# A gated scan with a soft mixture of experts: inputs laid out by numpy, one pool of 48 slots, phases of four units, a combine over 32 rows

## The chip, the cores and the metric

The kernel runs on one core of a Trainium2 chip. The metric is the device time of one execution in microseconds; 300.68 us is the median of three runs before the change. TensorE (PE) multiplies and transposes, VectorE (DVE), ScalarE (ACT) and GpSimd (POOL) compute, SyncE (SP) issues the DMA transfers.

## The reference

Four sequences of 5056 tokens with 256 channels pass a gated linear recurrence; its 20224 x 256 output is the input of a soft mixture of 8 experts with 4 slots each. Everything is fp32.

```python
a_base = sigmoid(a_param)
log_a  = 8 * sigmoid(r_gate) * log(clip(a_base))
a_t    = exp(log_a)
xg     = sqrt(max(1 - a_t*a_t, 1e-6)) * sigmoid(i_gate) * x
h[t]   = a_t[t] * h[t-1] + xg[t]            # scan over 5056 tokens: x for the second part

logits = x @ phi                            # [20224, 32 slots]
d      = softmax of logits over the tokens
slot_input = d.T @ x                        # [32, 256]
slot_out[e] = relu(slot_input[e] @ w1[e]) @ w2[e]      # 8 experts, 256 x 1024 x 256
c      = softmax of logits over the slots
out    = c @ slot_out                       # [20224, 256]
```

The output needs all tokens' logits and the slots' outputs, so there are two stages with a narrow place between them: gates, scan and the softmax sums over all tokens first, then a small expert MLP, then the combine and the stores.

## The kernel before, in words

Tokens are cut into quads of 512 (40, the last of 256) and units of two quads (21: the first unit has one quad, the last half a one). SBUF has 8 `st` buffers of 4 KB per partition, 20 `b` buffers of 8 KB, and a few small ones; PSUM has pairs of banks for the gate stage.

Names of tasks carry the quad, the unit (with channel half 0 or 1) or the group of up to four quads:

- `Dr`, `Di`, `Dx` (SP): loads of r_gate, i_gate and x, 512 KB each, tokens on partitions. `TR` (PE): transposes of r into PSUM, channels on partitions. `SR` (ACT, L797): tanh of it, from PSUM into `A`. `EX` (ACT, L865): exp, gives a_t; two whole units of a chunk can be taken by one instruction per half. `SQ` (POOL or DVE, L852): a_t squared, into `N`. `RT` (ACT, L888): the root.
- `SI` (ACT, L812): tanh of i_gate. `P1` (POOL, L823) and `U` (DVE L833, DVE or POOL L835): its product with x. The string `IV` gives a letter for each quad: D lets DVE do (tanh + 1) * x at once, P lets POOL add 1 first, E multiplies only and lets PE add x when it transposes, S uses the sigmoid table. `TU` (PE, L907): transposes of the product; under E both i and x pass through PE.
- `ST` (DVE, L925): the product times the root; `SC` (DVE, L942): the scan, in place in `A`. `TY` (PE), `YC` (DVE L981 or ACT L979): transposed back and copied out of PSUM.
- For each group: `LG` (PE, L1027) logits, `LE` and `LD` (running maximum over tokens), `TE`, `ES` (exp), `AC` (PE, sums weighted with it), `AE` (DVE). `CT`, `CM`, `CS`, `CE`, `RR`, `RB`, `RC`, `CN` make the softmax over the slots (transposes, maximum, subtraction, exp, sum, reciprocal, product); they can run in the gate stage or behind it.
- The narrow place: `MT`, `MX`, `MR`, `MC`, `WJ`, `WE`, `W`, `SP`, `SL` merge the sums into the slots' inputs; `L1` (PE, L1360), `HS`, `HT`, `HR`, `L2` (PE, L1408) are the MLP of all experts; `SO`, `RS` normalise and repeat the slots' outputs over the partitions.
- The combine: `CH`, `CL`, `SH`, `BD` split both factors into a high part of 12 mantissa bits and the rest, so that fp32r matmuls over 64 rows (32 slots of two parts) give the product: `HP` (PE, L1566) transposes, `HE` copies, `OT` (PE, L1593) multiplies, `OE` (DVE L1612, ACT L1610) copies out of PSUM, `OD` (SP, L1632) stores.

A planner in the file only turns these tasks into a program: the order on each engine is written out in the table `ORDER`, one list of names for an engine, and the buffers are given out in that order. PE gets filler transposes of the identity (L1231) where the plan has it idle. ACT needs a table load at each change between tanh or exp and the root, so the units are handled in chunks: all tanh and exp of a chunk, then all its roots. `CHUNKS` gives the number of units in each. On the chip each engine runs its list strictly in order and waits for the semaphores of its operands.

Of the kernel before, what the change touches and what calls it, by code (L numbers as in the profile page):

```python
# [1673 lines left out]
```

## Time and profile before

| | |
|---|---|
| runs | 300.63, 300.68, 301.33 us; median 300.68 |
| profiled execution | 300.78 us, of which the span of the core's instructions is 299.0 |
| busy | PE 267.0, DVE 243.1, ACT 247.1, POOL 189.0 us |
| moved | 78.94 MB read, 20.71 MB written |
| first store issued | 244.87 us after the span's start |

Busy time is that of instructions in execution. PE's includes fillers, and the ends of its matmuls are modelled, so a busy PE need not be at its limit. The share of DMA is the mean over 16 engines.

### The profile page before, as it was taken

Reading aid. Unit: us, or ns where it says so; the run is one execution under the profiler, and the core shown is the slowest. Engines: PE = TensorE matmul, PEld = TensorE weight load, DVE = VectorE, ACT = ScalarE, POOL = GpSimd, SP = SyncE. Lnnn points to the kernel's source line nnn. Section 1 sums busy time; section 2 is a strip of 40 time slices with the busy share of each in tenths; the row PEclk is TensorE's granted clock in tenths of the full one; section 3 lists DMA queues with packets and bytes.
Section 4 is the critical chain, followed back from the end, with each engine's and each line's share of the span. In section 5 each row is a group of like instructions: output and inputs, shape, how many; then the busy total and the mean of one; then the engine's idle time right before and its main releaser. Section 6 shows DMA issues by size and latency. Waiting matters only on the chain.

```text
span 299.0 us, 6623 instructions
## 1 busy us (share of the span) xinstructions
PE 267.0 (89%) x2657; PEld 211.4 (71%) x2657; DVE 243.1 (81%) x288; ACT 247.1 (83%) x275; POOL 189.0 (63%) x147
## 2 busy tenths in 40 slices
...
GB/s 237 416 409 386 406 409 409 299 339 333 409 258 353 340 302 382 278 385 300 226 287 301 365 215 353 377 426 346 362 401 295 0 55 392 413 414 419 419 407 264
DMA packets 23491, 100.08 MB, mean 335 GB/s; under 512 B 2850, under 2 KB 2852, under 8 KB 19364
## 3 DMA queue, kind: packets, MB, share of 16 engines
...
q10 hardware_dynamic: 4, 0.00, 0.0%
HBM read 78.94 MB, written 20.71 MB: 333 GB/s over the span
## 4 chain that ended last, share of the span: by engine, by line
ACT 39%; PE 29%; DVE 17%; issue 7%; DMA 3%; POOL 1%; ACTq 0%; DVEq 0%; POOLq 0%
ACT b L865 8%; ACT b L797 8%; ACT b L888 7%; DVE b L942 7%; ACT st L812 6%; PE bank L1593 6%; DVE pair L925 4%; DMA b<-in_moe_w_dram 3%; PE pair L907 3%; PE pair L786 3%; PE bank L1566 3%; PE bank L1408 2%; PE pair L965 2%; ACT L888 2%; ACT yn L979 2%
## 5 line engine op out<-in xcount | busy, mean ns | idle before, releaser
L852 POOL TENSOR_TENSOR b<-b 128x1024 f32<-128x1024 f32 (+2 forms) x40 | 72.6, 1833 | 29.6 <-ACT b L865 29.5
L925 DVE SCALAR_TENSOR_TENSOR pair<-b,pair 128x1024 f32<-128x1024 f32 (+2 forms) x42 | 48.1, 1156 | 4.3 <-PE pair L907 3.9
L965 PEld LDWEIGHTS pair<-ident,b 128*128 128x128 f32 x316 | 38.2, 194 | 13.2 <-ACT b L797 6.1
L942 DVE TENSOR_TENSOR_SCAN b<-b,b,pair 128x1024 f32<-128x1024 f32 (+3 forms) x24 | 47.2, 1974 | 0.3
L965 PE MATMUL pair<-ident,b 128*128 128x128 f32 x316 | 44.1, 284 | 2.8 <-ACT b L797 2.7
L786 PE MATMUL pair<-ident,st 128*128 128x128 f32 x316 | 42.3, 279 | 4.8 <-ACT b L797 2.3
L942 DVE TENSOR_TENSOR_SCAN b<-b,pair 128x1024 f32<-128x1024 f32 (+5 forms) x24 | 45.8, 1926 | 0.2
L907 PE MATMUL pair<-ident,b 128*128 128x128 f32 x316 | 43.2, 275 | 2.0 <-ACT b L797 1.1
L865 ACT ACTIVATE b<-b,ca 128x2048 f32<-128x2048 f32 (+3 forms) x28 | 44.3, 1607 | 0.1
L797 ACT ACTIVATE b<-pair 128x1024 f32<-128x1024 f32 (+1 forms) x40 | 40.3, 1018 | 4.3 <-PE pair L786 4.2
L786 PEld LDWEIGHTS pair<-ident,st 128*128 128x128 f32 x316 | 35.7, 143 | 10.6 <-ACT b L797 3.8
L907 PEld LDWEIGHTS pair<-ident,b 128*128 128x128 f32 x316 | 35.4, 140 | 6.1 <-ACT b L797 2.5
L835 POOL TENSOR_TENSOR b<-st,b 128x1024 f32<-128x1024 f32 (+1 forms) x17 | 39.3, 2319 | 0.2
L812 ACT ACTIVATE st<-st 128x1024 f32<-128x1024 f32 (+1 forms) x38 | 38.8, 1056 | 0.0
L888 ACT ACTIVATE b<-b 128x2048 f32<-128x2048 f32 (+2 forms) x21 | 36.9, 1804 | 0.1
L835 POOL TENSOR_TENSOR st<-st,b 128x1024 f32<-128x1024 f32 x12 | 28.8, 2403 | 8.1 <-ACT st L812 8.1
L1593 PE MATMUL bank<-bd,hT 64*128 64x256 f32 x232 | 27.5, 308 | 3.7 <-DVE hT L1579 1.5
L1593 PEld LDWEIGHTS bank<-bd,hT 64*128 64x128 f32 x232 | 21.6, 196 | 7.6 <-issue 2.1
L1027 PE MATMUL one<-b,phi_sb 128*32 128x256 f32 (+1 forms) x328 | 26.5, 419 | 0.0
L1231 PE MATMUL one<-ident 128*128 128x128 f32 x146 | 24.1, 283 | 1.4 <-POOL ident masks.py:199 1.4
L979 ACT COPY yn<-pair 128x1024 f32<-128x1024 f32 x22 | 22.2, 1018 | 1.3 <-PE pair L965 1.1
L1610 ACT COPY b<-bank 128x512 f32<-128x512 f32 x27 | 15.1, 597 | 9.5 <-PE bank L1593 7.7
...
## 6 DMA issues: line engine op xcount, KB each, us to landing
...
```

The lines of the kernel that those rows point to most:

```text
L786: nc.tensor.transpose(out=o[:, m, :], in_=raw("r", q)[:, m * D + h * P : m * D + (h + 1) * P], identity=ident,)
L797: nc.scalar.activation(dst, t(rp)[:, :, :c], AF.Tanh, scale=0.5)
L812: nc.scalar.activation(v, v, AF.Tanh, scale=0.5)
L835: eng.tensor_tensor(out=o, in0=a, in1=b, op=ALU.mult)
L852: eng.tensor_tensor(out=t(Nb[p])[:, h, :c], in0=v, in1=v, op=ALU.mult)
L865: nc.scalar.activation(v, v, AF.Exp, scale=ca[:, h : h + 1], bias=ca[:, h : h + 1])
L888: nc.scalar.activation(v, v, AF.Sqrt, bias=f, scale=-f)
L907: nc.tensor.matmul(o[:, m, :], raw(nm, q)[:, m * D + h * P : m * D + (h + 1) * P], ident, is_transpose=True, start=(nm == nms[0] and m == ...
L925: nc.vector.scalar_tensor_tensor(v, w, 1e-3 if gate_of(quads(p)[0]) == "S" else 0.5e-3, v, op0=ALU.max, op1=ALU.mult)
L942: nc.vector.tensor_tensor_scan(dst, dst, flat()[:, s0:s1], init, op0=ALU.mult, op1=ALU.add)
L965: nc.tensor.transpose(out=flat()[:, b * D + h * P : b * D + (h + 1) * P], in_=token(t(A[p])[:, h, : plen(p)], p)[:, :, (b0 + b) * len(quad ...
L1593: nc.tensor.matmul(t(ops[k])[:, m // 2 * D : (m // 2 + 1) * D], t(hT)[r, (b + m) * P // 2 : (b + m + 2) * P // 2], T["bd"][part][r, 0, :], ...
```

## The change

Numpy, ahead of the program, now lays the inputs out. r_gate comes by channel for each unit, so `TR` is gone and one load puts it straight into `A`, where `SR` works in place on 2048 columns. x and i_gate come by unit and by blocks of 128 tokens: a partition holds the tokens p, 128 + p and so on, so `TU`, `TY` and `LG` read and write contiguous blocks, and the output rows are put back in order by numpy at the end. Loads are 1 MB for a unit. w2, phi and a_param are rearranged too, and `L1` reads w1 contiguously.

`st` and `b` become one tile `all_s` of 48 slots of 4 KB; buffers take 1, 2 or 4 neighbouring slots, in an order that a further list `B` fixes. `CHUNKS` goes from nine to seven, of up to four units. `IV` has 18 quads of E in place of 12, 16 of P in place of 15, 6 of D in place of 11 and none of S. All lists of `ORDER` are new. A small subtraction `PD` on POOL stands ahead of `DM`.

The combine has no split any more: the 32 coefficients of each of a quad's four blocks lie on 32 partitions of one transposed tile (`TB`), and `OT` multiplies each block with plain fp32 matmuls over 32 rows, four row groups into four banks. `SW` copies the repeated slot outputs once. `OD` stores a unit at a time, and the half-size unit 0 is stored first.

```diff
-CHUNKS = [2, 2, 3, 3, 3, 3, 2, 2, 1]
+CHUNKS = [1, 3, 4, 4, 4, 4, 1]
...
-IV = 'DDDDDDEDDPPEDEPDPPEPEEPPEEPEPPEDPPEEPSSP'
+IV = 'PDEPDPDPPEEEEEEEEDEEEEEEEDDPEEPPPPPPPPPP'
...
-N_ST = 8
-N_B = 20
+N_S = 48
...
-        "CA SQ0.1 SQ1.1 U0 ST0.1 ST0.0 SC0.1 SC0.0 U2 U1 YC0.0 ST1.1 SC1.1 U4 ST1.0 SC1.0 U7 U3 YC2.0 ST2.1 ST2.0 U5 "
...
+        "CA U0 SQ1.1 SQ1.0 U4 SQ2.0 ST0.1 SC0.1 U1 ST0.0 SC0.0 ST1.0 ST1.1 SC1.0 SC1.1 U6 YC1.0 ST2.1 SC2.1 ST2.0 SC2.0 "
...
-EX2 = True
+EXG = 2
...
+        all_s = sb.tile([P, N_S, J * D], F32, name="all_s")
...
+    A = {p: Buf("s", f"A{p}", 2) for p in range(NP)}
+
+    def load(nm, p):
+        b = A[p] if nm == "r" else Buf("s", f"{nm}{p}", len(quads(p)))
+        c, tok0 = plen(p), pos_u(p) * QT
+
+        def emit():
+            rows = src[nm][tok0 : tok0 + c, :].rearrange("(p n) d -> p (n d)", n=c // P)
+            if nm == "r":
+                rows, dst = rows.rearrange("p (h c) -> p h c", h=H), t(b)[:, :, :c]
+                for h in range(H) if p == 0 else [slice(0, H)]:
+                    nc.sync.dma_start(out=dst[:, h], in_=rows[:, h])
+            elif len(quads(p)) > 1:
+                nc.sync.dma_start(out=t(b), in_=rows.rearrange("p (i f) -> p i f", i=2))
+            else:
+                nc.sync.dma_start(out=t(b)[:, : c // P * D], in_=rows)
...
-        def e_tr():
-            for h in range(H):
-                o = inv(t(rp)[:, h, :c], n)
-                for m in range(n):
-                    nc.tensor.transpose(
-                        out=o[:, m, :],
-                        in_=raw("r", q)[:, m * D + h * P : m * D + (h + 1) * P],
-                        identity=ident,
-                    )
-
-        tr = add("PE", f"TR{q}", 0.232 * n - (0.35 if q == 0 else 0), deps=[ld[("r", q)], t_const], prio=q - TRP, emit=e_tr,
-                 alloc=[rp], uses=[st[("r", q)]], shape="T")
+    def mk_sr(p):
+        c = plen(p)
 
         def e_sr():
-            dst = t(A[p])[:, :, i * QT : i * QT + c]
-            nc.scalar.activation(dst, t(rp)[:, :, :c], AF.Tanh, scale=0.5)
-
-        SR[q] = add("ACT", f"SR{q}", 0.06 + 0.85 * c / QT, deps=[tr], prio=q - 2, emit=e_sr,
-                    alloc=[A[p]] if i == 0 else [], uses=[rp] + ([A[p]] if i else []), kind="tanh")
+            v = t(A[p])[:, :, :c]
+            nc.scalar.activation(v, v, AF.Tanh, scale=0.5)
...
-            v = T["b2"][A[p].slot[0] // 2][:, h::2, :] if len(us) == 2 else t(A[p])[:, h, :c]
+            v = t(A[p])[:, h, :c]
+            if len(us) > 1:
+                v = all_s[:, A[p].slot[h] :][:, : 2 * len(us) - 1 : 2, :]
...
-                                o[:, m, :],
+                                t(up)[:, i, m * P : (m + 1) * P],
...
                         o = t(lp)[NS * j : NS * (j + 1), c0 : c0 + w]
-                        v = token(t(A[p])[:, h, : plen(p)], p)
-                        near = p >= WIDE_FROM
                         nc.tensor.matmul(
-                            o.rearrange("s (p i) -> s p i", p=P) if near else o.rearrange("s (i p) -> s i p", p=P), phi_sb[:, h, :],
-                            v[:, :, j * w // P : (j + 1) * w // P] if near else v[:, :, j::nb].rearrange("c p i -> c i p"),
+                            o.rearrange("s (i p) -> s i p", p=P), phi_sb[:, h, :],
+                            t(A[p])[:, h, : plen(p)].rearrange("c (i j p) -> c j i p", j=nb, p=P)[:, j],
...
-                        t(hp)[32 * j : 32 * j + NS, :FJ].rearrange("q (p f) -> q p f", f=FH), slots(e, h),
-                        wpart(wts[("w1", e)][0], h).rearrange("d (p j f) -> d j p f", j=J, f=FH)[:, j],
+                        t(hp)[32 * j : 32 * j + NS, :FJ], slots(e, h), wpart(wts[("w1", e)][0], h)[:, j * FJ : (j + 1) * FJ],
...
-    a = add("DVE", "SH", 0.35, deps=[a], prio=-60, uses=[sr], alloc=[soHb], emit=lambda: nc.vector.tensor_scalar(
-        t(soHb)[:, :D].bitcast(I32), t(sr)[:, :D].bitcast(I32), HIGH, None, op0=ALU.bitwise_and))
-
-    def e_b(part):
-        dst = T["bd"][part][:, 0, :]
-        if part:
-            nc.vector.tensor_tensor(out=dst, in0=t(sr)[:, :D], in1=t(soHb)[:, :D], op=ALU.subtract)
+
+    def e_rc():
+        if planner.cur.eng_used == "ACT":
+            nc.scalar.copy(out=t(soRb)[:, :D], in_=t(sr)[:, :D])
         else:
-            nc.scalar.copy(out=dst, in_=t(soHb)[:, :D])
-
-    t_bd = [add("DVE" if part else "ACT", f"BD{part}0", 0.35, deps=[a, t_bz], prio=-60, uses=[soHb, bdb] + ([sr] if part else []),
-                emit=lambda part=part: e_b(part)) for part in range(2)]
-
-    planner.warm_late = lambda pl: LATE and SC[(NP - 1, 0)].start is not None and t_bd[0].start is None
+            nc.vector.tensor_copy(out=t(soRb)[:, :D], in_=t(sr)[:, :D])
+
+    t_sw = add(("DVE", "ACT"), "SW", 0.35, deps=[a], prio=-60, uses=[sr], alloc=[soRb], emit=e_rc, alt={"ACT": 0.31})
...
-        k = add("POOL", f"CL{g}", 1.0, deps=[k], prio=pr, uses=[hl, lSb[g // 4]],
-                emit=lambda: nc.gpsimd.tensor_tensor(
-                    out=parts()[:, :, 1, :], in0=cn(), in1=parts()[:, :, 0, :], op=ALU.subtract))
...
+        def e_tb(n=n, rows=rows, ht=ht, g=g):
+            for k in range(n):
+                nc.tensor.transpose(
+                    out=t(ht)[:rows, k * P : (k + 1) * P], in_=lS(g)[:, k * rows : (k + 1) * rows], identity=ident)
...
+            def e_ot(m=m, k0=k0, ops=ops, hT=hT):
+                for k in range(m):
+                    for j, op in enumerate(ops):
+                        r = slice(NS * j, NS * (j + 1))
+                        nc.tensor.matmul(
+                            t(op)[:, k * D : (k + 1) * D], t(hT)[r, (k0 + k) * P : (k0 + k + 1) * P], t(soRb)[r, :D],
+                            start=True, stop=True)
+
+            k = add("PE", f"OT{p}", OTD * m, deps=[he, t_sw], prio=pr, emit=e_ot, alloc=ops, uses=[hT, soRb], shape="F")
+            ev = []
...
+            def e_od(p=p, og=og):
+                a0, c = quads(p)[0] * QT, per_part(p)
+                nc.sync.dma_start(
+                    out=out[a0 : a0 + plen(p), :].rearrange("(p n) d -> p (n d)", n=c), in_=t(og) if len(quads(p)) > 1 else t(og)[:, : c * D])
...
+def _spans(n):
+    q = J * P
+    return [(0, q)] + [(a, min(a + 2 * q, n)) for a in range(q, n, 2 * q)]
+def _by_unit(a):
+    flat = a.reshape(-1, a.shape[-1])
+    return _np.concatenate([flat[u:v].reshape(-1, P, a.shape[-1]).transpose(1, 0, 2).reshape(-1) for u, v in _spans(len(flat))]).reshape(a.shape)
+def _by_channel(a):
+    flat = a.reshape(-1, a.shape[-1])
+    return _np.concatenate([flat[u:v].reshape(v - u, -1, P).transpose(2, 1, 0).reshape(-1) for u, v in _spans(len(flat))]).reshape(a.shape)
+def _from_units(a):
+    return _np.concatenate([a[u:v].reshape(P, -1, a.shape[-1]).transpose(1, 0, 2).reshape(-1, a.shape[-1]) for u, v in _spans(len(a))])
...
+        if name in ("x", "i_gate"):
+            a = _by_unit(a)
+        elif name == "r_gate":
+            a = _by_channel(a)
+        elif name == "moe_w2":
+            a = _np.ascontiguousarray(a.reshape(a.shape[0], -1, P, a.shape[2]).transpose(0, 2, 1, 3)).reshape(a.shape)
+        elif name in ("a_param", "moe_phi"):
+            a = _np.ascontiguousarray(a.reshape(2, P, -1).transpose(1, 0, 2)).reshape(a.shape)
...
-    return got[0]
+    return _from_units(got[0])
```

What the lists move is shown at three places. On ACT, at the start of the program, behind the loads of the first table; L797 (L781 in the change) is `SR`, L865 (L850) `EX`, L812 (L796) `SI`, L888 (L864) `RT`. Before:

```order
L797 ACTIVATE b_69<-pair_92 128x2x512
L865 ACTIVATE b_69<-b_69,ca 128x512 x2
L797 ACTIVATE b_69<-pair_94 128x2x512
L797 ACTIVATE b_69<-pair_92 128x2x512
L812 ACTIVATE st_64<-st_64 128x1024
L865 ACTIVATE b_69<-b_69,ca 128x1024 x2
L797 ACTIVATE b_72<-pair_92 128x2x512
L888 ACT_TABLE_LOAD
L888 ACTIVATE b_70<-b_70 128x2x512
L888 ACTIVATE b_71<-b_71 128x2048
```

With the change:

```order
L850 ACTIVATE all_s<-all_s,ca 128x512 x2
L781 ACTIVATE all_s<-all_s 128x2048
L850 ACTIVATE all_s<-all_s,ca 128x1024 x2
L781 ACTIVATE all_s<-all_s 128x2048 x2
L796 ACTIVATE all_s<-all_s 128x1024
L850 ACTIVATE all_s<-all_s,ca 128x2x1024
L796 ACTIVATE all_s<-all_s 128x2048
L850 ACTIVATE all_s<-all_s,ca 128x2x1024
L796 ACTIVATE all_s<-all_s 128x2048
L864 ACT_TABLE_LOAD
L864 ACTIVATE all_s<-all_s 128x2x512
L864 ACTIVATE all_s<-all_s 128x2048 x3
```

The first root moves from behind two units, one of them the small one, to behind four units; `SR` and `SI` become 2048 columns wide.

On DVE, behind the last scan; L1043 (L1015) is `LE`, L1063 (L1035) `LD`, L1116 (L1089) `AE`, L981 `YC`, L1508 (L1443) `RR`, L1425 and L1428 of the change `CM` and `CS`. Before:

```order
L1063 TENSOR_SCALAR lD_84<-one_88,M 128x256
L1042 COPY M<-M 32x1 x2
L1043 TENSOR_SCALAR b_75,M<-one_87,M 64x128
L1063 TENSOR_SCALAR lD_83<-one_87,M 64x128
L1116 SCALAR_TENSOR_TENSOR accS<-accS,dm,one_88 128x257
L1292 TENSOR_REDUCE mmax<-one_87 1x32
L1294 COPY mrep<-mmax 1x128
L981 COPY yn_82<-pair_94 128x2x256
L1298 TENSOR_TENSOR wj<-M,one_87 128x1
L1508 TENSOR_REDUCE rs_all<-b_70 128x16
L1302 TENSOR_SCALAR W<-R,wj 128x128
L1116 SCALAR_TENSOR_TENSOR accS<-accS,dm,bank_2391 128x257
```

With the change:

```order
L1443 TENSOR_REDUCE rs_all<-all_s 128x16 x2
L1014 COPY M<-M 32x1 x2
L1015 TENSOR_SCALAR all_s,M<-one_70,M 64x128
L1089 SCALAR_TENSOR_TENSOR accS<-accS,dm,one_71 128x257
L1035 TENSOR_SCALAR lD_66<-one_70,M 64x128
L1250 TENSOR_REDUCE mmax<-bank_2017 1x32
L1425 TENSOR_REDUCE rm_79<-bank_2015 128x16
L1252 COPY mrep<-mmax 1x128
L1425 TENSOR_REDUCE rm_78<-bank_2019 128x16
L1089 SCALAR_TENSOR_TENSOR accS<-accS,dm,one_71 128x257
L1428 TENSOR_TENSOR all_s<-bank_2019,rm_78 128x512
L1256 TENSOR_TENSOR wj<-M,bank_2017 128x1
```

Two sums over rows of groups done earlier, two maxima and a subtraction now stand in the stretch up to the weights of the merge, and a copy of `YC` has gone from it.

On PE, the first matmuls of the combine; in the first list eight of them make one quad (`bd` is the split matrix, `hT` the transposed coefficients), in the second the operands are plain fp32 tiles. Before:

```order
L1593 MATMUL bank_2391<-bd_2493,hT_2495 128x256
L1593 MATMUL bank_2396<-bd_2493,hT_2495 128x256
L1593 MATMUL bank_2391<-bd_2494,hT_2495 128x256
L1593 MATMUL bank_2396<-bd_2494,hT_2495 128x256
L1593 MATMUL bank_2391<-bd_2493,hT_2495 128x256
L1593 MATMUL bank_2396<-bd_2493,hT_2495 128x256
L1593 MATMUL bank_2391<-bd_2494,hT_2495 128x256
L1593 MATMUL bank_2396<-bd_2494,hT_2495 128x256
```

With the change (L1497 is `OT`, L1471 `TB`):

```order
L1497 MATMUL bank_2017<-all_s,eS_69 128x256
L1497 MATMUL one_71<-all_s,eS_69 128x256
L1497 MATMUL bank_2019<-all_s,eS_69 128x256
L1497 MATMUL bank_2018<-all_s,eS_69 128x256
L1497 MATMUL bank_2017<-all_s,eS_69 128x256
L1497 MATMUL one_71<-all_s,eS_69 128x256
L1497 MATMUL bank_2019<-all_s,eS_69 128x256
L1497 MATMUL bank_2018<-all_s,eS_69 128x256
L1471 MATMUL bank_2016<-ident,all_s 128x128 x4
```

A unit of one quad now takes four matmuls into four banks; the next row shows transposes of another group between units.

## Rows read from the trace of the kernel before

**Rows 1.** The page: busy time of each engine, and GB/s in 40 slices of 7.5 us.
```profile
PE 267.0 (89%) x2657; PEld 211.4 (71%) x2657; DVE 243.1 (81%) x288; ACT 247.1 (83%) x275; POOL 189.0 (63%) x147
...
GB/s 237 416 409 386 406 409 409 299 339 333 409 258 353 340 302 382 278 385 300 226 287 301 365 215 353 377 426 346 362 401 295 0 55 392 413 414 419 419 407 264
```

**Rows 2.** Stages: from:to, length, busy us (x instructions) by engine, PE clock, DMA share, GB/s.
```profile
0.00:25.00 25.00, 22.78 (x174) 21.89 (x175) 8.09 (x10) 20.33 (x21) 6.45 (x31) 1.00 0.93 360
...
25.00:217.35 192.35, 181.18 (x1752) 143.85 (x1751) 187.28 (x168) 189.67 (x181) 160.49 (x93) 1.00 0.90 339
...
217.35:245.00 27.65, 26.96 (x370) 16.96 (x368) 17.25 (x54) 9.23 (x20) 11.66 (x11) 1.00 0.44 182
...
245.00:299.00 54.00, 36.07 (x367) 28.72 (x365) 30.44 (x59) 27.86 (x56) 10.41 (x13) 0.83 0.94 385
```

**Rows 3.** Groups on ACT by shape: out<-in xcount | busy us, mean ns | idle before.
```profile
L797 ACT ACTIVATE b<-pair 128x1024 f32<-128x1024 f32 x39 | 39.7, 1028 | 4.3 <-PE pair L786 4.2
...
L812 ACT ACTIVATE st<-st 128x1024 f32<-128x1024 f32 x37 | 38.2, 1068 | 0.0
...
L888 ACT ACTIVATE b<-b 128x2048 f32<-128x2048 f32 x19 | 35.3, 1905 | 0.1
...
L865 ACT ACTIVATE b<-b,ca 128x2048 f32<-128x2048 f32 x14 | 29.5, 2113 | 0.1
...
L979 ACT COPY yn<-pair 128x1024 f32<-128x1024 f32 x22 | 22.2, 1018 | 1.3 <-PE pair L965 1.1 <-ACT rs_all L1503 0.2
...
L888 ACT ACT_TABLE_LOAD x9 | 11.5, 1283 | 0.2
...
L1496 ACT ACTIVATE b<-b 128x512 f32<-128x512 f32 x8 | 5.1, 635 | 0.0
```

**Rows 4.** Groups on DVE by shape, and one of POOL, same columns.
```profile
L925 DVE SCALAR_TENSOR_TENSOR pair<-b,pair 128x1024 f32<-128x1024 f32 x38 | 46.0, 1219 | 3.5 <-PE pair L907 3.0 <-ACT b L888 0.3
...
L981 DVE COPY yn<-pair 128x1024 f32<-128x1024 f32 x17 | 20.6, 1215 | 0.6 <-PE pair L965 0.5
...
L833 DVE SCALAR_TENSOR_TENSOR b<-st,b 128x1024 f32<-128x1024 f32 x11 | 14.0, 1285 | 2.2 <-ACT st L812 2.2
...
L852 DVE TENSOR_TENSOR b<-b 128x1024 f32<-128x1024 f32 x1 | 1.9, 1881 | 6.6 <-ACT b L865 6.6
...
L1490 DVE TENSOR_REDUCE rm<-one 128x16 f32<-128x512 f32 x7 | 4.7, 670 | 0.0
...
L835 POOL TENSOR_TENSOR b<-st,b 128x1024 f32<-128x1024 f32 x16 | 38.0, 2384 | 0.2
```

**Rows 5.** Order of time at the start: start us, us, engine line op out<-in.
```profile
5.99 1.02 ACT L797 ACTIVATE b<-pair 128x1024 f32<-128x1024 f32 x1 [1.90 <-PE pair L786]
...
7.05 1.52 ACT L865 ACTIVATE b<-b,ca 128x512 f32<-128x512 f32 x2
...
12.83 2.37 ACT L865 ACTIVATE b<-b,ca 128x1024 f32<-128x1024 f32 x2
...
17.42 2.86 ACT L888 ACTIVATE b<-b 128x1024 f32<-128x1024 f32 x2
...
19.12 1.29 DVE L925 SCALAR_TENSOR_TENSOR pair<-b,pair 128x512 f32<-128x512 f32 x2 [0.87 <-PE pair L907]
```

**Rows 6.** Order of time from the last scan to the first stores (DVE, PE, SP).
```profile
216.60 0.75 DVE L942 TENSOR_TENSOR_SCAN b<-b,b,pair 128x256 f32<-128x256 f32 x1
...
229.11 2.95 PE L1360 MATMUL bank<-b,yn 128*32 128x256 f32 x48
...
236.50 2.80 PE L1408 MATMUL bank<-b,b 128*32 128x256 f32 x48
...
243.34 1.22 PE L1593 MATMUL bank<-bd,hT 64*128 64x256 f32 x16 [0.35 <-ACT bd L1438]
...
244.87 3.38 SPq L1632 DMA_DIRECT2D out_dram<-st  x4
```

**Rows 7.** A stretch late in the stores, columns as in the stages.
```profile
280.00:285.00 5.00, 3.59 (x25) 2.63 (x23) 2.30 (x5) 1.94 (x4) 0.00 (x0) 0.60 1.01 415
```

More of the change, by code (lines that the diff above doesn't have):

```diff
@@ L186 @@
         "eng", "name", "dur", "lat", "deps", "prio", "alloc", "uses", "emit",
-        "kind", "start", "end", "left", "outs", "seq", "eng_used", "alt", "shape", "gate", "lock",
+        "kind", "start", "end", "left", "outs", "seq", "eng_used", "alt", "shape", "gate", "lock", "parts",
     )
@@ L437, in tag_for @@
                 continue
-            if b.mate is not None and self.twin() is None:
+            if g == "s":
+                if self.run_of(b.need["s"] * len(b.group or [b])) is not None:
+                    return g
                 continue
@@ L444, in tag_for, with run_of @@
         return None
-    def twin(self):
-        free = self.slots["b"]
-        return next((i for i in free if i % 2 == 0 and i + 1 in free), None)
+    def run_of(self, n):
+        free = {k: i for i, k in enumerate(self.slots["s"])}
+        best, least = None, None
+        for k in free:
+            if n > 1 and (k % 2 or any(k + m not in free for m in range(1, n))):
+                continue
+            old = max(free[k + m] for m in range(n))
+            if n == 1:
+                cost = 200 * ((k ^ 1) in free) + 100 * ((k ^ 2) in free and (k ^ 3) in free) - k
+            elif n == 2:
+                cost = 100 * ((k ^ 2) in free and (k ^ 3) in free) + old
+            else:
+                cost = 100 * (k % 4) + old
+            if least is None or cost < least:
+                best, least = k, cost
+        return best
     def filler(self, now):
@@ new lines, in raw, with side_by_side @@
+    def raw(nm, q):
+        p, i = unit[q]
+        return t(st[(nm, q)])[:, i, :] if len(quads(p)) > 1 else t(st[(nm, q)])
+    Nb = {(p, h): Buf("s", f"N{p}.{h}") for p in range(NP) for h in range(H)}
+    def side_by_side(bufs):
+        for b in bufs:
+            b.group = bufs
+    wide, first_of = [], {}
+    for ch in chunks:
+        full = [p for p in ch if plen(p) == 2 * QT]
+        wide += [full[k : k + EXG] for k in range(0, len(full), EXG)]
+        wide += [[p] for p in ch if p not in full]
@@ L760 @@
+    for us in wide:
+        first_of.update(dict.fromkeys(us, us))
+        if len(us) > 1:
+            side_by_side([A[p] for p in us])
+    for p in range(NP):
+        side_by_side([Nb[(p, h)] for h in range(H)])
     yn = {q: Buf("yn", f"yn{q}") for q in range(NQ)}
```

543 lines of the change are left out of this document (208 added, 335 removed), and 108 rows, old and new, of the table ORDER.

## The prediction

> **What bounds the kernel now.** I read the page's busy line first, then the stages, then the instruction groups of the two engines that are never idle, then the order of time at the start, at the hand-over and at the first stores. The busy line gives PE, DVE and ACT more than 80% each [rows 1], and cannot say which one binds. The stages can [rows 2]. I cut at 25 us, at 217.35 (the end of the last scan, 216.60 + 0.75 [rows 6]) and at 245 (the first store goes out at 244.87 [rows 6]).
>
> In the gate stage, 25 to 217.35 us, DVE is busy 187.28 of 192.35 us and ACT 189.67; DMA moves 339 GB/s, where it can do some 410 [rows 1]. So VectorE and ScalarE bind together, 5.07 and 2.68 us idle, and DMA only follows. Before 25 us DVE has worked 8.09 us and waited 16.91: its first scaling of a unit (ST) starts at 19.12, behind the first roots [rows 5]. PE looks full (181.18), but many of its matmuls are fillers on the identity; its load shows in one place, the 3.0 us that DVE waited for L907 in front of its ST group [rows 4].
>
> From 217.35 to 245 a serial chain of small steps runs, with DMA at 0.44. From the first store on, DMA is busy at 0.94 over the whole stretch and at 1.01 late in it, while DVE works 30.44 and ACT 27.86 of 54 us [rows 2, 7]: stores bind there. The sum is therefore: end of the last scan, plus hand-over, plus stores. The profiled execution took 300.78 us for a span of 299.0, so 1.78 lie outside; it is 0.1 above the median 300.68.
>
> **The gate stage, DVE.** Up to the end of the last scan DVE works 8.09 + 187.28 = 195.4 us. The lists change its tasks up to there so: U 11 to 7 (4 x 1.285 = -5.1), YC 17 to 13 (4 x 1.215 = -4.9), CM and CS together 16 to 10 (6 x 0.67 = -4.0, CS taken as CM), RR 4 to 1 (3 x 0.67 = -2.0, as CM of the same shape) [rows 4]. These last are not removed but moved behind the scan. SQ goes from one half and one whole squaring to four whole ones. The whole one took 1.881 [rows 4]; an undisturbed one should be near the 1.219 of an equally large two-input operation [rows 4]. Four cost 4.9 to 7.5; I take 1.5 each, 6.0, since POOL runs beside them, against about 2.5 now: +3.5. Sum -12.5: DVE has 182.9 us of work.
>
> The Trainium skill speaks against this item: GPSIMD Engine Reference, section 1 Specifications, says that POOL shares its SBUF interface with VectorE and that the two contend when a DVE instruction has two SBUF inputs, as a squaring has. The 1.881 beside 1.219 agrees; with that price for all four, DVE would have 1.5 us more.
>
> **The start.** The first phase now holds units 0 to 3 before the first root. ACT's queue by rows: the first r tanh began at 5.99 behind transposes that are gone; take 5.0. Then SR0 1.03, EX0 1.52, SR3 1.9, EX3 2.37, SR2 and SR1 3.8, SI0 1.07, the pair's exponentials 2 x 2.11 with SI2 and SI1 3.8 between and behind, the table 1.28, RT0 1.07 [rows 3, 5]. That is 27.1 us; a 2048-wide tanh from SBUF is priced as the 2048-wide root, 1.905 [rows 3]. Loads do not hold it: the eight transfers up to i of unit 1 are 6.8 MB, and the slices 237, 416, 409 GB/s of 7.5 us [rows 1] bring them by 20 us, while ACT asks for the last at 22.8. So ST0 starts at 27.1 instead of 19.12. DVE can do about 7.4 us of U, SQ and constants ahead, and idles 19.7 us there.
>
> From 27.1 it has 175.5 us left. If it waits as before (5.07 of 192.35), the last scan ends at 207.4; if the 3.0 us behind PE go because the 316 r transposes are gone, at 204.5.
>
> **The gate stage, ACT.** 20.33 + 189.67 = 210.0 us now, to the same point. SR: 40 reads of a PSUM pair at 1.028 become 19 of 1.905 and two small ones, -2.4. SI: 39 at 1.068 and a half become the same, -3.0. YC 22 to 27: +5.1. CE: six of seven leave the stage, 6 x 0.635 = -3.8. Table loads fall from 21 to 16: -6.4 [rows 3]. Two more paired exponentials are left out of the sum. 199.3 us; with the 7.35 us that it idled before (4.67 up to 25 us and 2.68 behind), 206.7.
>
> The Trainium skill (ScalarE: Activation LUTs, What ACT_TABLE_LOAD costs) has 1283 ns for the load and another 1380 for a drain at every switch. The row has the 1283 and 0.2 us of idle ahead of nine loads; the drain does not show. With it, five switches would give 13.3, not 6.4, and ACT would be out of the way at about 200.
>
> Both engines need each other's results, so I take the later end: **last scan at 207**, 10.3 earlier. Range 203 to 212.
>
> POOL takes four more U's (4 x 2.384 = 9.5 [rows 4]) and about two squarings fewer: up to 170 us of the 180 that remain behind 25 us. PE loses 316 transposes, gains 48 for the additional E gates. Neither binds in the sum. Loads and stores carry the same bytes; slots are 48 of 4 KB per partition either way (8 + 20 x 2). Two 1 MB loads replace four halves: no gain counted where DMA isn't the bound.
>
> **The hand-over.** Now 244.87 - 217.35 = 27.5 us. The new DVE list puts RR5, RR2, CM4, CM6 and CS6 between the last scan and SL, where YC39 and RR6 stood: five of 0.67 against about 0.6 + 0.67 (YC39 is of half size), +2.1 at most; some will fall into waits for PE, so +1.6. All matmuls of the expert MLP wait behind SL. L1 reads its weights contiguously: 48 matmuls in 2.95 against L2's 2.80 with contiguous operands [rows 6]; 128 of them, -0.4. The split of the combine matrix (SH, BD) becomes one copy, but HE0 and a reciprocal stand ahead of that copy in DVE's list and two transposes groups ahead of RS on PE: I count nothing. **28.7 us**; first store at 235.7.
>
> **The stores.** 299.0 - 244.87 = 54.1 us, 20.7 MB at the rate of DMA. The combine per block of 512 tokens (quad) changes from eight fp32r matmuls of 64 rows to four fp32 ones of 32 rows, which the trace counts as two instructions each, so eight again. Four narrow ones abreast take 2.80 / 12 = 0.233 per round [rows 6], and a quad needs two rounds: 0.47 us on PE, 19 for all; copies out of PSUM stay at 80-odd; HE halves; CH and CL go. DMA needs 1.25 us per quad (49.5 / 39.5). Hidden: **54.1 stays**. End of span 289.8, time **291.6**; I say 291.5, with a range of its own of 288 to 295.
>
> **The rivals.**
> *Slower: the 32-row matmuls run one after another.* No row shows four row groups at once. The 64-row pairs do overlap (16 in 1.22 [rows 6]). One after another a quad is 8 x 0.233 = 1.87, and 39.5 quads 74 us instead of 54: 235.7 + 74 + 2 + 1.8 = 313. It decides from 1.25 us per quad on. A half overlap (0.93) would stay hidden. The Trainium skill (TensorE: Matmul & The Clock Gate, Part 3) states that MMs in distinct 32-row groups run concurrently, measured 3.07 times as fast at N = 512; no run shown here can confirm it, and by it the quad is near 0.6 us and hidden. Chance 0.07. A sister of it is the clock: late in the stores it stands at 0.6 over 5 us [rows 7], as PE's work thins, and PE will have less now; at half clock a quad is 0.93 plus transposes, still about DMA's 1.25: 2 us at most.
>
> *Phases of four starve DVE.* Roots of a chunk wait for the squarings of four units on a POOL that is busy 170 of 180; if one 1.9 us piece is late at three of the five chunks, the last scan comes 5 or 6 us later: 296 to 299.5. For it: ST0 starts 8 us later already, and POOL's idle reserve goes. Against it: DVE idled only 5 us in 192 with POOL, ACT and PE all in its way. Chance 0.14.
>
> *Better.* The PE waits vanish (204.5) and the five row operations fall into waits of the hand-over (27.1): 204.5 + 27.1 + 54.1 + 1.8 = 287.5; down to 284.5 if DVE also starts early. Chance 0.17.
>
> *No change* (within 0.3%, which is about what a measurement of this kernel can tell): the saving is eaten by starvation of 10 us. Chance 0.05. Other slowdowns, such as late weights ahead of L1 or buffers that come free late in the shared pool: 0.05.
>
> **How the numbers follow.** Forecast 0.52, better 0.17, starved 0.14, no change 0.05, slower 0.07 + 0.05. Faster 0.83, same 0.05, slower 0.12. The range 285 to 299 leaves out the slower cases, most of no change and the lower tip of the better one.
>
> **What would show it.** ST0 near 27 us with 16 table loads in all; DVE and ACT at 97% from there; last scan near 207; first store 28 to 29 us behind it; 54 us of stores with DMA near 1.0, and OT quads near 0.5 us. I am wrong if DVE's idle time between 27 us and the last scan passes 8 us, if OT quads take over 1.25 us, or if L1 waits for weights.

## The result, and the profile after

The changed kernel takes 291.3 us (median of four runs, 290.14 to 292.62) against 300.65 before: a ratio of 0.9694, 95% interval 0.9636 to 0.9751. On the chip of the first experiments it was 290.62 us and 0.9663 (0.9636 to 0.9690). The forecast was 291.5. The profiled execution took 292.1 us for a span of 290.3. Two executions that took longer at a lower granted clock are left out of all ratios below; one is the profiled one of the kernel with both sets of copies shortened (294.0 us beside 289.1 to 291.7), so its trace isn't read.

The page after: busy time of each engine, and in 40 slices the granted PE clock in tenths.

```profile
PE 239.7 (83%) x2415; PEld 183.5 (63%) x2415; DVE 234.8 (81%) x273; ACT 232.0 (80%) x219; POOL 189.0 (65%) x150
...
PEclk9999689779999997999999999999999999999655
```

The stages after, cut where [rows 2] is cut: at 25 us, at the end of the last scan (209.86) and at the first store (237.08); columns as there.

```profile
0.00:25.00 25.00, 23.64 (x191) 23.65 (x192) 6.19 (x5) 21.50 (x17) 13.23 (x35) 1.00 0.93 381
25.00:209.86 184.86, 154.41 (x1510) 118.51 (x1512) 179.63 (x155) 180.47 (x138) 164.36 (x100) 0.95 0.90 366
209.86:237.08 27.22, 26.76 (x380) 16.85 (x369) 20.44 (x62) 8.63 (x25) 5.82 (x8) 1.00 0.19 77
237.08:290.30 53.22, 34.93 (x347) 24.51 (x345) 28.56 (x55) 21.45 (x43) 5.63 (x7) 0.81 0.95 390
```

Of the 8.7 us of span, 7.5 come from the last scan (217.35 to 209.86), 0.3 from the hand-over (27.52 to 27.22) and 0.9 from the stores (54.13 to 53.22). All four engines are busy for 84 to 98% of the second row, and the clock has dropped to 0.95 in a stage where it had stood at 1.00.

DVE after, in order of time: the squarings and products ahead of the first ST, the first ST, two products behind it, two waits for PE, and the last scan.

```profile
21.13 2.91 DVE L835 TENSOR_TENSOR all_s<-all_s 128x1024 f32<-128x1024 f32 x1
23.97 1.21 DVE L835 TENSOR_TENSOR all_s<-all_s 128x1024 f32<-128x1024 f32 x1
25.10 1.21 DVE L816 SCALAR_TENSOR_TENSOR all_s<-all_s 128x1024 f32<-128x1024 f32 x1
26.24 1.21 DVE L835 TENSOR_TENSOR all_s<-all_s 128x1024 f32<-128x1024 f32 x1
27.89 0.69 DVE L899 SCALAR_TENSOR_TENSOR pair<-all_s,pair 128x512 f32<-128x512 f32 x1 [0.43 <-ACT all_s L864]
29.75 2.08 DVE L816 SCALAR_TENSOR_TENSOR all_s<-all_s 128x1024 f32<-128x1024 f32 x1
34.82 1.23 DVE L899 SCALAR_TENSOR_TENSOR pair<-all_s,pair 128x1024 f32<-128x1024 f32 x1 [1.12 <-PE pair L881]
37.74 1.23 DVE L899 SCALAR_TENSOR_TENSOR pair<-all_s,pair 128x1024 f32<-128x1024 f32 x1 [1.69 <-PE pair L881]
...
43.37 2.46 DVE L816 SCALAR_TENSOR_TENSOR all_s<-all_s 128x1024 f32<-128x1024 f32 x1
...
209.12 0.74 DVE L916 TENSOR_TENSOR_SCAN all_s<-all_s,pair 128x256 f32<-128x256 f32 x1
```

POOL meanwhile, in order of time: a squaring up to 22.97, nothing up to 26.60, then its own products.

```profile
20.09 2.88 POOL L835 TENSOR_TENSOR all_s<-all_s 128x1024 f32<-128x1024 f32 x1
26.60 3.06 POOL L818 TENSOR_TENSOR all_s<-all_s 128x1024 f32<-128x1024 f32 x1 [3.64 <-DMA all_s<-in_x_dram]
29.65 1.11 POOL L806 TENSOR_SCALAR all_s<-all_s,one_sb 128x1024 f32<-128x1024 f32 x1
30.85 3.22 POOL L818 TENSOR_TENSOR all_s<-all_s 128x1024 f32<-128x1024 f32 x1
...
42.36 2.38 POOL L818 TENSOR_TENSOR all_s<-all_s 128x1024 f32<-128x1024 f32 x1
```

Groups by shape, from the start to the end of the last scan, first of DVE (U, SQ, YC), then of ACT (SR, SI, YC); they answer to [rows 3] and [rows 4].

```profile
L955 DVE COPY yn<-pair 128x1024 f32<-128x1024 f32 x13 | 15.8, 1212 | 0.1
L816 DVE SCALAR_TENSOR_TENSOR all_s<-all_s 128x1024 f32<-128x1024 f32 x6 | 9.5, 1592 | 0.0
L835 DVE TENSOR_TENSOR all_s<-all_s 128x1024 f32<-128x1024 f32 x4 | 6.8, 1730 | 0.0
...
L781 ACT ACTIVATE all_s<-all_s 128x2048 f32<-128x2048 f32 x19 | 35.9, 1907 | 1.1 <-DMA all_s<-in_r_gate_dram 1.1
L796 ACT ACTIVATE all_s<-all_s 128x2048 f32<-128x2048 f32 x19 | 35.8, 1902 | 0.0
L953 ACT COPY yn<-pair 128x1024 f32<-128x1024 f32 x26 | 25.8, 1006 | 1.5 <-PE pair L939 1.5
```

ACT in order of time, ahead of the first root: each instruction begins about 0.1 us before its predecessor has ended (17.80 + 2.08 = 19.88, and the next starts at 19.79).

```profile
17.80 2.08 ACT L850 ACTIVATE all_s<-all_s,ca 128x2048 f32<-128x2048 f32 x1
19.79 1.90 ACT L796 ACTIVATE all_s<-all_s 128x2048 f32<-128x2048 f32 x1
21.59 2.09 ACT L850 ACTIVATE all_s<-all_s,ca 128x2048 f32<-128x2048 f32 x1
```

PE and SP after, at the hand-over and in the first combine.

```profile
218.15 3.66 PE L1315 MATMUL one<-all_s,yn 128*32 128x256 f32 x64
...
235.33 0.91 PE L1497 MATMUL bank<-all_s,lD 32*128 32x256 f32 x9
235.87 0.38 PE L1497 MATMUL one<-all_s,lD 32*128 32x256 f32 x2
236.09 0.38 PE L1497 MATMUL one<-all_s,lD 32*128 32x256 f32 x2
236.30 0.38 PE L1497 MATMUL one<-all_s,lD 32*128 32x256 f32 x2
...
237.08 13.48 SPq L1521 DMA_DIRECT2D out_dram<-all_s  x8
```

The `one` rows are one row group's passes, 0.21 us apart, with the three other groups' passes between them: four narrow matmuls run abreast, a quad needs two rounds, 0.43 us.

### The profile page after: what moved, and what is told of

It reads as the page before. It is cut to its first block, busy times and chain, and to the rows that moved or that the text cites. A ratio compares the mean times of both kernels' runs of the same rounds, so it can differ in the third digit from the quotient of the medians.

```text
span 290.3 us, 5894 instructions
## 1 busy us (share of the span) xinstructions
PE 239.7 (83%) x2415; PEld 183.5 (63%) x2415; DVE 234.8 (81%) x273; ACT 232.0 (80%) x219; POOL 189.0 (65%) x150
## 4 chain that ended last, share of the span: by engine, by line
PE 23%; DVE 13%; POOL 8%; ACT 6%; DMA 5%; issue 4%; DVEq 0%; SPq 0%; ACTq 0%; POOLq 0%
DVE all_s L916 5%; PE bank L1497 4%; POOL all_s L818 4%; PE pair L881 4%; DVE pair L899 3%; DMA out_dram<-all_s 3%; DMA all_s<-in_moe_w_dram 2%; PE bank L1361 2%; PE one L1497 2%; POOL all_s L835 2%; ACT all_s L796 2%; PE pair L939 2%; PE bank L1471 2%; ACT all_s L781 1%; PE one L1315 1%
## 5 line engine op out<-in xcount | busy, mean ns | idle before, releaser
L916 DVE TENSOR_TENSOR_SCAN all_s<-all_s,pair 128x1024 f32<-128x1024 f32 (+8 forms) x48 | 92.7, 1950 | 0.6
L818 POOL TENSOR_TENSOR all_s<-all_s 128x1024 f32<-128x1024 f32 (+1 forms) x33 | 78.4, 2391 | 3.8 <-DMA all_s<-in_x_dram 3.6
L835 POOL TENSOR_TENSOR all_s<-all_s 128x1024 f32<-128x1024 f32 (+2 forms) x38 | 70.6, 1879 | 11.8 <-ACT all_s L850 7.0
L881 PE MATMUL pair<-ident,all_s 128*128 128x128 f32 x460 | 62.8, 291 | 17.0 <-DVE all_s L916 10.1
L881 PEld LDWEIGHTS pair<-ident,all_s 128*128 128x128 f32 x460 | 54.7, 149 | 25.6 <-issue 8.6
L899 DVE SCALAR_TENSOR_TENSOR pair<-all_s,pair 128x1024 f32<-128x1024 f32 (+2 forms) x42 | 48.1, 1153 | 4.2 <-PE pair L881 3.4
L939 PE MATMUL pair<-ident,all_s 128*128 128x128 f32 x316 | 43.6, 282 | 4.9 <-DVE yn L955 2.4
L939 PEld LDWEIGHTS pair<-ident,all_s 128*128 128x128 f32 x316 | 34.8, 143 | 15.4 <-DVE all_s L916 4.1
L850 ACT ACTIVATE all_s<-all_s,ca 128x2048 f32<-128x2048 f32 (+3 forms) x24 | 42.1, 1788 | 0.2
L864 ACT ACTIVATE all_s<-all_s 128x2048 f32<-128x2048 f32 (+2 forms) x21 | 37.2, 1806 | 2.4 <-POOL all_s L835 2.3
L781 ACT ACTIVATE all_s<-all_s 128x2048 f32<-128x2048 f32 (+2 forms) x21 | 37.6, 1807 | 1.1 <-DMA all_s<-in_r_gate_dram 1.1
L796 ACT ACTIVATE all_s<-all_s 128x2048 f32<-128x2048 f32 (+2 forms) x21 | 37.4, 1801 | 0.0
L953 ACT COPY yn<-pair 128x1024 f32<-128x1024 f32 (+1 forms) x27 | 26.4, 991 | 2.2 <-PE pair L939 2.2
L1074 PE MATMUL one<-yn,eS 128*32 128x257 f32 x316 | 23.2, 387 | 3.7 <-DVE accS L1087 2.2
## 6 DMA issues: line engine op xcount, KB each, us to landing
all_s<-in_x_dram SPq DMA_DIRECT2D x1, 512.0 KB, 14.7
```

Of the source, the lines that this page charges most:

```text
L781: nc.scalar.activation(v, v, AF.Tanh, scale=0.5)
L796: nc.scalar.activation(v, v, AF.Tanh, scale=0.5)
L818: eng.tensor_tensor(out=o, in0=a, in1=b, op=ALU.mult)
L835: eng.tensor_tensor(out=t(Nb[(p, h)])[:, :c], in0=v, in1=v, op=ALU.mult)
L850: nc.scalar.activation(v, v, AF.Exp, scale=ca[:, h : h + 1], bias=ca[:, h : h + 1])
L864: nc.scalar.activation(v, v, AF.Sqrt, bias=f, scale=-f)
```

## The experiments

Theory A was that DVE and ACT bind the gate stage together, so that the gain is the work taken from both. Its rivals: B, ACT alone binds; C, DVE alone; D, the gain came from PE, which lost the transposes of r. Each kernel below is the changed one with one edit, which can move its line numbers by a few, and each ratio is to the kernel before on the same chip. "Stage" means from the first ST to the end of the last scan: 182.0 us in the profile above and 180.7 in the repeat. Executions of one kernel lie 1 to 3 us apart, so smaller differences between two profiles of the stage say nothing.

**Again.** No edit.

> The changed kernel once more, on the chip of the next three, as their measure. Every theory: 290 to 292.5 us, last scan near 210 us, DVE waiting 2.8 us for PE between 34 and 38 us.

290.62 us, ratio 0.9663 (0.9636 to 0.9690). Last scan at 208.2; DVE's waits for PE at that place were 0.7 and 0.2 us this time. The stage holds 177.0 us of DVE's work and 177.6 of ACT's in 180.7.

**PE kept awake.** From 26.5 to 29.9 us PE stands still behind a filler that waits for a bank read by the first scan; its clock is 0.51 from 34 to 38 us. The edit keeps the fillers off such banks and makes them longer.

```diff
+        if 22.2 < now < 33.0 and g == "pair":
+            g = None
...
-        for _ in range(2):
+        for _ in range(5 if 22.2 < planner.cur.start < 29.5 else 2):
```

> The changed kernel, with the filler transposes between the first units' transposes and ST0 kept off the banks that wait for a scan, and five transposes long instead of two. In the changed kernel PE stood still from 26.3 to 29.9 us, its granted clock was 0.50 from 32 to 38, and DVE then waited 1.1 and 1.7 us for the transposes of units 1. Theory A (DVE and ACT bind together through the gate stage, whatever either loses at its head is lost at its end): the clock stays at 1.0, both waits go, the last scan comes 1 to 2.8 us earlier, 288.5 to 290.5 us; a full 2.8 if DVE alone binds. Rival B (ACT alone binds and DVE's waits are taken from slack): the waits go, and the last scan stays within 0.5 us of 209.9.

Measured 290.42 us, 0.9657 (0.9630 to 0.9684): no change. Stretches of 4 us (columns as in the stages), first of the changed kernel, then of this one.

```profile
26.00:30.00 4.00, 0.58 (x6) 0.34 (x5) 3.53 (x5) 3.99 (x4) 3.40 (x2) 1.00 1.01 422
30.00:34.00 4.00, 3.31 (x20) 3.07 (x21) 3.66 (x3) 3.98 (x3) 3.92 (x2) 0.64 1.01 422
34.00:38.00 4.00, 4.00 (x21) 4.00 (x20) 1.49 (x2) 3.99 (x3) 1.41 (x3) 0.51 1.01 416
```

```profile
26.00:30.00 4.00, 4.00 (x39) 4.00 (x38) 3.52 (x4) 3.99 (x4) 4.00 (x2) 1.00 1.01 418
30.00:34.00 4.00, 4.00 (x39) 4.00 (x38) 3.38 (x4) 3.97 (x4) 3.62 (x2) 1.00 1.01 420
34.00:38.00 4.00, 2.83 (x27) 2.59 (x26) 3.83 (x3) 4.00 (x3) 1.94 (x2) 1.00 1.02 424
```

The clock stays at 1.00, and the first twelve transposes of unit 1 take 1.47 us instead of 2.82. The two waits add up to 0.8 us. But the repeat, without the edit, had 0.9 there: the 2.8 of the first profile belong to one execution, in which the clock stood at 0.50 from 32 to 37 us, and in the repeat only from 30 to 33. Against the repeat the stage is 180.4 us instead of 180.7, so the low clock at this place costs nothing that shows. Whether waits of 2.8 us would cost anything stays open.

**Unit 0's root first.** Its loads, squarings and products move forward with it (in lists not shown); the buffers keep their slots.

Each list is shown from its start to its last change.

```diff
-"SA LN SR0 EX0.1 EX0.0 SR3 EX3.0 EX3.1 SR2 SR1 SI0 EX1.1 SI2 EX1.0 SI1 RT0.0 RT1.0
+"SA LN SR0 EX0.1 EX0.0 SR3 SI0 RT0.0 EX3.0 EX3.1 SR2 SR1 EX1.1 SI2 EX1.0 SI1 RT1.0
...
-"CA U0 SQ1.1 SQ1.0 U4 SQ2.0 ST0.1 SC0.1 U1 ST0.0 SC0.0 ST1.0
+"CA U0 ST0.1 SC0.1 ST0.0 SC0.0 U4 SQ1.1 SQ1.0 SQ2.0 U1 ST1.0
```

> The changed kernel with unit 0's root ahead of units 1 to 3 (two more table loads, 2.57 us on ACT), its loads, squarings and products moved forward to suit, every buffer in the slots it had. ST0 can then start at about 16 us instead of 27.9, and 3.9 us of DVE's work falls into its idle time at the start. If DVE alone binds: 1 to 4 us faster (3.9 less what units 1 to 3 come later). If ACT alone binds: 2 to 2.6 us slower. Theory A: the two nearly cancel, within 2 us, on the slower side. The prediction priced the late ST0 at 8 us of DVE's time; if that price was real, this run is faster.

Measured 293.6 us, 0.9761 (0.9732 to 0.9791): 1.0% or 3.0 us slower. DVE in order of time:

```profile
15.91 0.70 DVE L905 SCALAR_TENSOR_TENSOR pair<-all_s,pair 128x512 f32<-128x512 f32 x1 [0.82 <-PE pair L887]
...
26.23 1.23 DVE L822 SCALAR_TENSOR_TENSOR all_s<-all_s 128x1024 f32<-128x1024 f32 x1 [6.53 <-ACT all_s L802]
...
35.87 2.47 DVE L905 SCALAR_TENSOR_TENSOR pair<-all_s,pair 128x1024 f32<-128x1024 f32 x2 [1.69 <-PE pair L887]
```

The first ST came at 15.91, 12 us earlier, and bought nothing: the last scan ended at 211.84, 3.6 later than in the repeat. DVE then waited 6.53 us for ACT's tanh of i, and its first ST of a whole unit came at 35.87, in the repeat at 34.08. ACT had worked 2.75 us more (18 table loads) and waited 0.95 longer for r, together 3.7. This fits an end that hangs on ACT from the start on. It does not show what a late first ST costs by itself, since the edit also lengthens ACT's list ahead of all that follows.

**Hand-over.** Two sums, two maxima and a subtraction moved off the way to the merge.

```diff
-LE10 LD10 RR5 RR2 LE11 AE9 LD11 MX CM4 MR CM6 AE10 CS6 WJ AE11 W SL RR6
+LE10 LD10 LE11 AE9 LD11 MX MR CM4 AE10 WJ CM6 AE11 W CS6 SL RR5
```

(This is a piece of DVE's list. RR2, RR6 and RR1 stand a few places further on to suit.)

> The changed kernel with RR5, RR2, CM4, CM6 and CS6 taken from between the last scan and the weights of the merge: the two sums move behind SL, CM4 and CM6 behind the copy they delayed, CS6 behind W. The prediction priced the five at 1.6 us of the hand-over: if so, the first store comes 1.0 to 1.6 us after the last scan earlier than 27.2 us. Rival: they lie in waits for PE (MC stands behind AC11, and DVE waited 1.0 us ahead of SL), and the hand-over shrinks by 0.5 us at most, total time unchanged within 0.3%.

Measured 291.53 us, 0.9700 (0.9663 to 0.9738); from the last scan to the first store 27.09 us instead of 27.22 (27.21 to 27.23 in the runs above and in those on ACT and DVE below, which leave this part alone). Taking the five away brings 0.1 us, not 1.6, which fits operations that lie in waits.

**More work on ACT.**

```diff
+            if p in (7, 11, 15):
+                nc.scalar.preload_act_table_set("natural_log_exp_and_others")
+                nc.scalar.preload_act_table_set("exp_and_others")
```

> The changed kernel with two table loads more behind SR7, SR11 and SR15, six in all: 7.7 us of ACT's time, the reverse of the fall from 21 to 16 loads. Theory B (ACT alone sets the pace): +6.5 to +7.7 us, 297 to 298.5. Theory A (ACT and DVE bind together): +5.5 to +7.7. Theory C (DVE alone): under +2.

Measured 297.59 us, 0.9879 (0.9812 to 0.9946), 2.2% above the changed kernel's 0.9663. The stage is 187.6 us, 6.9 longer for 7.4 of ACT's time.

**More work on DVE.**

```diff
                     nc.vector.tensor_copy(out=dst, in_=v)
+                    if q in (4, 5, 8, 11, 18, 21):
+                        nc.vector.tensor_copy(out=dst, in_=v)
```

> The changed kernel with the DVE copies YC4, YC5, YC8, YC11, YC18 and YC21 made twice: 6 x 1.21 = 7.3 us of DVE's time, about what CM, CS, RR and YC had lost in the gate stage. Theory A: +5.5 to +7.3, 296 to 298. Theory C: +6.5 to +7.3. Theory B: up to the 3.4 us that DVE waits in the stage are taken first, so +3 to +4 at most if its waits can be filled, 293.5 to 294.5.

Measured 298.47 us, 0.9926 (0.9895 to 0.9958), 2.7% more. The stage is 187.9, 7.2 longer for 7.1 of DVE's. Theories B and C, one engine alone, fall.

**Less on ACT; less on DVE; less on both.** In the three, only 32 of 256 columns are copied for the named quads; the edit for ACT is shown, the others differ in the list of quads:

```diff
+                if q in (15, 16, 17, 19, 22, 25, 27):
+                    dst, v = dst[:, :, :32], v[:, :, :32]
```

> The changed kernel with seven of ACT's copies (YC15, 16, 17, 19, 22, 25, 27) shortened from 256 to 32 columns of each block, the rest of yn left as it was: some 5 us less work on ACT between 110 and 170 us, nothing else changed. Theory B: 4 to 5 us faster, 285.5 to 286.5. Theory A: 0 to 1.5 faster, since DVE is then in the way. Theory C: no change.

> The changed kernel with six of DVE's copies (YC7, 8, 11, 18, 21, 24) shortened from 256 to 32 columns of each block, the rest of yn left as it was: some 5.5 us less work on DVE. Theory C: 4.5 to 5.5 us faster, 285 to 286. Theory A: 0 to 1.5 faster, ACT being in the way. Theory B: no change.

> The changed kernel with both sets of shortened copies: seven of ACT's and six of DVE's, 4.5 and 5.6 us of work less, the rest of yn left as it was. One alone brought 0.9 us (ACT) and nothing (DVE). Theory A (both engines bind together): from ST0 to the last scan 176 to 177.5 us instead of 180.7, 286 to 287.5 in all. Rival: a third engine (POOL, 178.6 us of work in 208) or the waits between them hold the stage anyway, and it stays at 179.5 or more.

Measured 289.73 us, 0.9635 (0.9554 to 0.9717), for ACT; 292.02, 0.9701 (0.9614 to 0.9787), for DVE; 291.52, 0.9688 (0.9638 to 0.9738), for both. By these intervals none differs from the changed kernel. The third was to be 1.1 to 1.6% faster, so theory A in its simple form falls as well.

Where ACT's 4.5 us went, as far as two profiles tell: its list of waits in the stage, first of the repeat, then of this kernel.

```profile
ACT yn L953 <- PE pair L939: 1.5, 4, 0.7
ACT all_s L864 <- POOL all_s L835: 1.0, 2, 0.6
```

```profile
ACT yn L955 <- PE pair L939: 3.5, 7, 1.0
ACT all_s L864 <- POOL all_s L835: 2.2, 3, 1.1
```

ACT's idle time in the stage rose from 3.05 to 6.54 us: it now waits for TY on PE and for squarings on POOL. Where DVE's 5.6 us went: 2.9 of them were eaten by its six U, 1994 ns each where the repeat had 1513, since they now meet POOL at work, and its idle time rose by 3.9.

```profile
L816 DVE SCALAR_TENSOR_TENSOR all_s<-all_s 128x1024 f32<-128x1024 f32 x6 | 11.9, 1994 | 0.0
```

**PE's load of before put back, in another place.**

```diff
-                for b in range(nb):
+                for b in [*range(nb)] * 2:
```

> The changed kernel with every transpose of TY made twice into the same place: 316 transposes more, as many as r needed before, 34 us of PE at full clock. Theory A: PE has room (177 us in 208, of which fillers are part), so the stage grows by 1.5 us at most, 290 to 292.5. Rival D (the change gained because PE was relieved of r's transposes): +3 to +7, 294 to 298.

Measured 307.82 us, 1.0272 (1.0211 to 1.0333): 17 us slower than the changed kernel, and slower than before. The stage is 196.1 us. DVE's largest waits in it, and ACT's:

```profile
DVE yn L955 <- PE pair L939: 6.2, 5, 2.9
DVE pair L899 <- PE pair L881: 5.6, 8, 1.4
DVE rm L1425 <- PE one L1412: 3.0, 3, 1.4
...
ACT yn L953 <- PE pair L939: 13.3, 16, 1.4
```

PE has no room of that size where it stands between DVE's scans and the copies; the expectation of 1.5 us at most was wrong, and so was rival D's 7. The r transposes stood ahead of the tanh, with ACT's queue to hide them, so 17 us is not what their removal was worth. Rival D is neither shown nor excluded; only that PE had this time to spare at this place is excluded.

**Squarings back on POOL.** SQ1.1, SQ1.0, SQ2.0 and SQ5.1 moved from DVE's list to POOL's, and the order `B` of the slots with them; 113 of 153 buffers then lie elsewhere.

> The changed kernel with the four squarings on DVE (SQ1.1, SQ1.0, SQ2.0, SQ5.1) on POOL, as nearly all were before. Theory A: three of the four lie in DVE's idle time ahead of ST0, so DVE gains 1.2 to 2 us only, while 5.7 us more on POOL hold up the first roots and the products behind them: 0.5 to 3 us slower, 291.5 to 294. The prediction's sum charged DVE 6.0 us for the four; if that were on the path the run would be 2 to 5 us faster.

Measured 297.13 us, 0.9909 (0.9879 to 0.9939), 2.5% slower; the expectation had 3 us at most. One row of ACT's waits says that something else came in:

```profile
ACT all_s L781 <- DMA all_s<-in_r_gate_dram: 5.8, 3, 3.2
```

Loads of r came late, which they had not (0.8 us in the repeat, at the start); that the other slots are the reason is likely but not shown. DVE waited 3.3 us for a load of x, which it had not, and more for PE too (5.0 us instead of 1.9). What the placement of the squarings is worth by itself stays open.

**Combine one after another.**

```diff
-                        r = slice(NS * j, NS * (j + 1))
+                        r = slice(0, NS)
```

> The changed kernel with all four blocks of a quad multiplied from the coefficients and slot outputs on partitions 0 to 31, so that no two matmuls have row groups of their own; three of four output blocks then hold the first block's values. If the four row groups run abreast only because they are distinct, a quad takes 8 x 0.233 = 1.87 us, more than the 1.25 us of DMA, and the stores grow from 53.2 to 74 to 76 us: 311 to 314. If not, nothing changes: 290 to 292.5.

Measured 391.75 us, 1.3055 (1.2975 to 1.3136). The stores take 154 us, twice the expectation. Two sets of four passes in order of time, and the stretches from the first combine on (columns as in the stages):

```profile
236.93 1.02 PE L1497 MATMUL one<-all_s,lD 32*128 32x256 f32 x4
237.80 1.02 PE L1497 MATMUL bank<-all_s,lD 32*128 32x256 f32 x4
```

```profile
234.67:240.00 5.33, 5.33 (x25) 4.42 (x24) 1.54 (x3) 1.77 (x6) 0.71 (x1) 0.96 0.24 98
240.00:245.00 5.00, 5.00 (x16) 3.73 (x15) 0.69 (x1) 1.14 (x3) 0.00 (x0) 0.50 0.51 210
...
250.00:300.00 50.00, 50.00 (x131) 37.84 (x131) 8.14 (x19) 7.26 (x14) 4.33 (x5) 0.50 0.31 126
```

At full clock a pass took 0.22 us (four from 236.93 to 237.80), near the 0.233 it was priced at; from 240 us on the granted clock was 0.50 and a pass 0.43. A quad is then 8 x 0.43 = 3.4 us, and 39.5 quads 136; transposes at the same clock and gaps make up the rest.

## Why the prediction was right, and where it was not

**The sum held, term by term within 3 us.** Last scan 207 forecast, 209.86 and 208.2 measured; hand-over 28.7 against 27.2; stores 54.1 against 53.2; span 289.8 against 290.3 and 288.7. The errors partly cancel, and the step from the work of two engines to the end of the stage did not hold in the runs (below), so that the sum came this close is in part luck.

**DVE's work: 182.9 forecast, 185.8 measured.** YC (15.8), CM, CS and RR came as priced. The seven U were mis-sized: 7 x 1.285 = 9.0 forecast, 11.6 measured (9.5 for six on L816, 2.05 for U0), because more of them now start while POOL works (4 of 7, before 3 of 11). The rows above show it directly. The squaring at 23.97 and the product at 25.10, with POOL idle, take 1.21 us. The squaring at 21.13, the product at 29.75 and that at 43.37 start while an instruction of POOL runs; they take 2.91, 2.08 and 2.46, and each ends some 1.08 us behind the end of POOL's (24.04 behind 22.97, 31.83 behind 30.76, 45.83 behind 44.74). The squaring at 26.24 starts ahead of POOL's product at 26.60 and takes 1.21; POOL's takes 3.06 instead of 2.38. So in these rows the one that starts later waits for the other. So the Trainium skill's rule weighed for SQ (GPSIMD Engine Reference, section 1 Specifications) holds for U as well, which also reads two inputs from SBUF; I used it for SQ and not for U. The price of 1.5 for SQ was low (1.73).

**ACT's work: 199.3 forecast, 202.0 measured.** The prediction's own terms add up to 199.5, a slip of 0.2. 16 table loads, SR and SI came as forecast by their rows. The step that failed was to take whole durations off the busy time: consecutive instructions overlap by about 0.1 us, and 47 fewer instructions give back less than their durations add up to (the durations fall by 14.7 us in all, the busy time by 8.0). CE was mis-sized too: four stayed in the stage, not one. That the drain which the Trainium skill (ScalarE: Activation LUTs, What ACT_TABLE_LOAD costs) adds does not bear here was borne out: six more loads raised ACT's work by 7.4 us (6 x 1.283 = 7.7), and the time by 6.5.

**The start.** ST0 at 27.1 forecast, 27.89 measured. But the sum through DVE, 27.1 and then 175.5 us of work, is not borne out: a first ST 12 us earlier brought no gain, as DVE then waited for ACT. The sum through ACT fits that run better (its 2.75 us of work and 0.95 of waiting more make up the 3.6 by which the last scan came later).

**"Neither binds in the sum", of PE and POOL, was wrong.** I added up two engines and dismissed the other two for being below 100%. Work added to ACT or DVE comes out nearly in full (6.9 of 7.4 us, 7.2 of 7.1); work added to PE in TY's place at 15.4 us of stage for 25.3 of busy time (152.8 to 178.1); and work taken from ACT, from DVE or from both brings nothing that shows. My reading is that the stage is one net of four engines at 84 to 98% whose fixed lists are cut for these durations, and that no engine's sum is its length. That neither ACT nor DVE alone nor the two together set its length is shown, within the intervals; what does is not. The sums may have been near because the new lists lower, up to the last scan, ACT by 8.0, DVE by 9.6 and PE by 25.9 us at once (POOL rises by 10.7). The share of each edit in the 7.5 us, that of the vanished r transposes above all, stays open: no run here undoes an edit with lists made for it. The rows of before have one hint: ACT waited 4.2 us for the transposes of r [rows 3] and now waits 1.1 for loads of r; but its idle time up to the last scan did not fall by it (7.4 us before, 7.9 now). Nor did a run test the clock's later falls in the stage (0.66 from 55 to 65 us).

**The hand-over.** The +1.6 for five inserted operations was mis-sized: they cost 0.1 us. L1 starts 8.3 us behind the last scan instead of 7.6, and L1's way to the first L2 takes 7.4 us instead of 8.4, more than the 0.4 that I gave contiguous weights; how much of that is the order of the weights is not shown.

**The stores.** The four row groups do run abreast, 0.43 us for a quad, and DMA stays the bound (0.95). By the rounds 0.21 us apart, against 0.22 for one pass alone, the gain over one after another is about fourfold at 256 columns; the Trainium skill (TensorE: Matmul & The Clock Gate, Part 3) has 3.07 at N = 512, which no run here has. Of the rivals, the serial one was mis-sized by its clock: 392 us, not 313. The fall of the clock late in the stores came (0.6 to 0.5 in the last three slices) and cost nothing that shows: 53.2 us against 54.1. Starvation did not come: DVE idled 4.8 us behind the first ST where 8 was the bound.
